# Attention over a few memory slots, then a maxout FFN: four token tiles divided, and a new order of pieces

## The chip, the cores and the metric

The kernel runs on one core of one Trainium2 chip. The metric is the time of one execution on the device in microseconds (us), the median of several runs. Lower is better. A profiled execution gives the trace; its times count from the first instruction (the start of the span).

## The reference, cut to what matters

Eight batches of eight heads, 576 tokens, head size 64, 32 memory slots per head. Keys and values are first gathered into the memory slots, the queries then attend to the slots, and an FFN without biases follows over all 4608 tokens.

```python
a = phi - np.max(phi, axis=2, keepdims=True)
a = np.exp(a)
a = a / (np.sum(a, axis=2, keepdims=True) + 1e-09)
k_m = np.einsum('bhsm,bhsd->bhmd', a, k)
v_m = np.einsum('bhsm,bhsd->bhmd', a, v)
scores = scale * np.matmul(q, k_m.transpose(0, 1, 3, 2))
scores = scores - np.max(scores, axis=-1, keepdims=True)
attn = np.exp(scores)
attn = attn / (np.sum(attn, axis=-1, keepdims=True) + 1e-09)
x = np.matmul(attn, v_m)          # then heads side by side: 4608 x 512
h = np.maximum(np.maximum(x @ w1, x @ w2), x @ w3)
return (h @ w_out).astype(np.float32)
```

## The kernel before

The kernel never forms `x`. The value memory of a batch (32 slots x 64 for each head) is multiplied into the weights, so that attention weights go straight into the FFN. With w1 and w2 the differences to w3 are used: the maximum of three becomes w3's part plus a maximum of two differences and zero, and w3's part reaches the output through w3 @ w_out.

All work is cut into pieces. A piece is a letter, sometimes a number, and a batch: F8@1 is piece F8 of batch 1. A list written out in the code gives the order in which the pieces are issued, and since each engine takes its instructions in program order, the list is the order of every engine's queue. The pieces that matter here:

- L0, L1, L2, L3: the loads of phi, k, v and q of a batch. They are issued by POOL (GpSimd). Loads take eight semaphores in turn, so a load waits until the eighth one before it has landed; it also waits until the buffer (two of each kind) is free. From batch 2 on, r0 and r1 (POOL, L109) copy k and v into a packed buffer.
- E: exp of phi (ACT, L235). B: memory of keys and values on PE (L255, 72 small matmuls); in batches 0 and 1 in two parts, B0 for keys, B1 for values. N: its normalization (DVE, L273 to L287). K: its transposition (PE, L302) and the copy of the result (kvt).
- Q0, Q1: transpositions of q (DVE, L317). S: scores (PE, L337, 32 matmuls) and their exp into e2, in two halves (ACT, L346).
- a, s, c, m, X: for each half of e2, transposition, sum, reciprocal (DVE, L391, L399, L408), multiplication (POOL, L413) and transposition back into `attn` (DVE, L421).
- D0 to D3 (PE, L444): the value memory times the weights ("fold"), copied into `wp` and `wp3` by ACT or DVE, with a star by both. V: the difference of w2 or w1 to w3 (DVE, L219).
- F0 to F11 (PE, L473, four matmuls each): the FFN's first layer for 128 features of one of the two differences. An even F is copied with Relu into `h1` (mostly ACT, L176), the odd F after it is combined with it into `hT` (DVE, L486).
- T0 to T4 (PE, L504 and L513): the second layer for 128 tokens: six matmuls on `hT` and two on `attn`, then a copy into `ot` (ACT or DVE) and an output transfer of 256 KB issued by SP (L534). T4 joins the halves of two batches; T3 of the last batch is done in two parts.

A mark "!" behind a piece gives its copy to the other of ACT and DVE.

PSUM has eight banks. A string of digits in the code names the bank for each piece in turn: one bank for a T or a K, two for a B, D or F, two times two for an S. A piece can start when the last reader of its bank is done.

The first part of the list, up to F4@0, does the start: warming matmuls, the memory of batch 0, the products of the weights. Behind it the tiles of batch 0 stand among the pieces of batch 1, those of batch 1 among the pieces of batch 2, and so on. Before the change a T is one piece, and the order in which its matmuls go through `hT` is that in which the odd F of the batch were issued (`fts`).

Of the kernel before, what the change touches and what calls it, by code (L numbers as in the profile page):

```python
# [15 lines left out]
def kernel(  # L16
# [24 lines left out]
    FT = DF // P  # L41
# [97 lines left out]
    for i in range(P // M):  # L139
# [4 lines left out]
    banks = iter(  # L144
        "".join(
            """
            02010240624567676476420642064204624062453605040462041642062402640150646025126026
            40246024076024764206560260426406246023062414216420640240624042612640234024620460
            24620462352604620520640260240640264204024601460424323232
            """.split()  # L150
        )
    )
# [1 line left out]
    def one_bank():  # L154
        return psum[:, int(next(banks))]
# [166 lines left out]
    attns = {}  # L322
# [137 lines left out]
    hts = {}  # L460
    fts = {}
# [28 lines left out]
                op=ALU.max,  # L490
            )

    osts = {}

    def ffn2(b, t, swap):


        hT, attn = hts[b // 2], attns[b // 2]
        c0 = S - HP if t == 4 else (b % 2) * (S + HP) + t * P
        if b == B - 1 and t == 3:  # L500
            return ffn2_last(b, c0)
        po = one_bank()
        for n, fc in enumerate(fts[b]):
            nc.tensor.matmul(  # L504
                po,
                lhsT=hT[:, fc, c0 : c0 + P],
                rhs=wo_sb[:, fc, :],
                start=(n == 0),
                stop=False,
            )  # L510
# [19 lines left out]
        ot = opool.tile([P, DM], FP32, name="ot")  # L530
        r0 = (b // 2) * 2 * S + c0
        rows = out[r0 : r0 + P, :]
        evacuate("T", t, swap, ot, po)
        nc.sync.dma_start(out=rows, in_=ot)  # L534

    def ffn2_last(b, c0):

        hT, attn = hts[b // 2], attns[b // 2]
        ot = opool.tile([P, DM], FP32, name="ot")
        r0 = (b // 2) * 2 * S + c0  # L540
        for i in range(2):
            c = (slice(0, DM - P), slice(DM - P, DM))[i]
            po = one_bank()[:, 0 : c.stop - c.start]
            for n, fc in enumerate(fts[b]):
                nc.tensor.matmul(  # L545
                    po,
                    lhsT=hT[:, fc, c0 : c0 + P],
                    rhs=wo_sb[:, fc, c],
                    start=(n == 0),
                    stop=False,  # L550
                )
            for g in range(NG):
                nc.tensor.matmul(
                    po,
                    lhsT=attn[:, g, c0 : c0 + P],
                    rhs=wp3s[b][:, g, c],
                    start=False,
                    stop=(g == NG - 1),
                )
            rows = out[r0 : r0 + P, c]  # L560
            if i == 0:
                nc.vector.tensor_copy(out=ot[:, c], in_=po)
                nc.sync.dma_start(out=rows, in_=ot[:, c])
            else:
                nc.scalar.copy(out=ot[:, c], in_=po)
                nc.scalar.dma_start(out=rows, in_=ot[:, c])

    def issue(b, n, swap):

        i = int(n[1:]) if len(n) > 1 else None  # L570
        {
            "I": lambda: [make_identity(nc, ident)]
            + [nc.gpsimd.memset(x[:, :, :, 2 * D : 2 * D + 1], 1.0) for x in kvrs],
            "Y": lambda: load_w(i) if i < 3 else load_wo(),
            "L": lambda: load_ph(b) if i == 0 else load_q(b) if i == 3 else load_kv(b, i - 1),
            "H": lambda: load_kv(b, i % 2, halves[i // 2]),
            "r": lambda: pack(b, i),
            "E": lambda: [att_exp(b, h) for h in (halves if b == 0 else [slice(0, NP)])],
            "B": lambda: att_kv(b, i),
            "N": lambda: att_kv_norm(b, i),  # L580
            "K": lambda: att_kv_t(b, swap, i),
            "Q": lambda: att_q(b, i),
            "S": lambda: att_score(b),
            "a": lambda: att_t(b, i),
            "s": lambda: att_sum(b, i),
            "c": lambda: att_rec(b, i),
            "m": lambda: att_mul(b, i, swap == "!"),
            "X": lambda: (ones_mul if (b, i) in ONES else att_back)(b, i),
            "M": lambda: ones_sum(b, i),
            "R": lambda: ones_rec(b, i),  # L590
            "D": lambda: fold(b, i, swap),
            "F": lambda: ffn1(b, i, swap),
            "T": lambda: ffn2(b, i, swap),
            "W": lambda: w3_t(i, swap),
            "O": lambda: w3_o(i, swap),
            "V": lambda: w_diff(i),
            "Z": lambda: warm_up(i),
        }[n[0]]()


    for w in """
        E@0 H2@0 H0@0 L3@0 Z25@0 B0@0 I@0 N0@0 Z2@0 K0@0! Q0@0 Q1@0 Z9@0 S@0 Z2@0 M0@0 M1@0 R0@0
        Y2@0 R1@0 W0@0 Y3@0 W1@0 W2@0 Z6@0 O1@0 H3@0 O3@0 O2@0 H1@0 X1@0 B1@0 X0@0 N1@0 K1@0
        O0@0 Y0@0 D1@0! D0@0! D3@0 F8@0 F10@0 F2@0 V0@0 F6@0 F0@0! Y1@0 D2@0 D4@0 L0@1 V1@0 F4@0
        F3@0 E@1 L1@1 F5@0 F11@0 F1@0 F7@0 F9@0 L3@1 B0@1 N0@1 L2@1 L1@2 Q0@1 Q1@1 T0@0 V2@0
        K0@1! T3@0 S@1 a0@1 T1@0 a1@1 L2@2 s0@1 L0@2 B1@1 N1@1 L3@2 c0@1 K1@1 m0@1 s1@1 c1@1
        D1@1* D0@1 m1@1 X0@1 X1@1 D2@1! L2@3 D3@1* T2@0 F8@1 L0@3 F10@1 L1@3 F6@1 r0@2 r1@2
        F4@1! F2@1 F9@1 F5@1 F0@1 E@2 F3@1 F11@1 F7@1 F1@1 L3@3 B@2 L2@4 T2@1! L1@4 N@2 K@2!
        T1@1 Q0@2 Q1@2 S@2 L0@4 T4@1! L3@4 a0@2 s0@2 c0@2 r1@3 a1@2 D1@2! E@3 m0@2 s1@2 c1@2
        D0@2* m1@2 D2@2 X0@2 X1@2 T0@1 T3@1 F10@2 F2@2 F6@2 F3@2 F7@2 F0@2 F11@2 r0@3 L1@5 F1@2  # L610
        Q0@3 D3@2 B@3 F8@2 N@3 F9@2 r1@4 F4@2 F5@2 L2@5 K@3! Q1@3 T2@2! S@3 D0@3 a0@3 r0@4 s0@3
        a1@3 E@4 T3@2 c0@3 s1@3 c1@3 T0@2! m0@3 D2@3* D1@3* m1@3 X1@3 L0@5 B@4 D3@3 T1@2 X0@3
        N@4 F6@3 F4@3 Q0@4 L0@6 F8@3 Q1@4 F5@3 F9@3 F0@3 F7@3 F2@3 F1@3 L3@5 F3@3 K@4! F10@3
        L3@6 F11@3 S@4 E@5 T3@3 a0@4 T0@3! L2@6 r0@5 a1@4 s1@4 s0@4 c0@4 r1@5 c1@4 m0@4 D2@4*
        B@5 D1@4! X0@4 D0@4* m1@4 L1@6 X1@4 L1@7 T1@3 F6@4 F4@4 N@5 K@5! F2@4 F8@4! F5@4 L2@7
        F10@4 L0@7 Q0@5 F7@4 Q1@5 F0@4 F1@4 F11@4 T2@3 S@5 F3@4 r1@6 F9@4 a1@5 s1@5 L3@7 T4@3
        E@6 c1@5 Q1@6 m1@5 a0@5 X1@5 D3@4 r0@6 D3@5* D1@5! s0@5 c0@5 T2@4! T3@4 Q0@6 D2@5* D0@5
        m0@5 B@6 T0@4! r0@7 N@6 X0@5 K@6 F10@5 F4@5! F2@5 F11@5 r1@7 F3@5 F6@5! F8@5 F5@5 F7@5
        F9@5 Q0@7 E@7 F0@5 F1@5 T1@4! S@6 B@7 D1@6! a0@6 N@7 s0@6 T3@5 K@7 Q1@7 T0@5 S@7 a1@6
        c0@6 s1@6 D3@7 c1@6 a1@7 m0@6 T1@5 s1@7 D2@6* m1@6 D0@6* D2@7 a0@7 X0@6 s0@7 T4@5! D1@7!  # L620
        c0@7 D0@7! X1@6 c1@7 m1@7 D3@6* T2@5! m0@7 F6@6 F10@6 X1@7 F7@6 F4@6 F0@6! X0@7 F8@6
        F2@6 F11@6 F5@6 F9@6 F4@7 F1@6 F8@7 F3@6 F6@7! T1@6! F5@7 F0@7! F1@7 F2@7 T0@6! T3@6
        F10@7 F7@7 F11@7 F3@7 T2@6 F9@7 T0@7! T1@7! T2@7 T4@7! T3@7
    """.split():
        n, b = w.rstrip("!*").split("@")
        issue(int(b), n, w[-1])
# [30 lines left out]
```

## Time and profile before

| | |
|---|---|
| median of 3 runs | 165.16 us (164.99 to 165.55) |
| the profiled execution | 165.26 us |
| its span, first to last instruction | 163.5 us |
| PE busy | 154.2 us (94%) |
| DVE, ACT, POOL busy | 108.7, 87.0, 69.5 us |
| granted TensorE clock | 1.0 |
| HBM read, written | 39.32, 9.44 MB |

PE is TensorE's matmuls, DVE VectorE, ACT ScalarE, POOL GpSimd, SP SyncE, which issues the outputs. Ends of matmuls are modelled, so PE's pace is read from the starts. In a row of the list in order of time stand the start and the length in us, the engine, the line, what is written and read, and how many instructions are merged; in brackets the idle time of the engine before it and what ended it.

### The profile page before, as it was taken

The numbers are of one execution on the slowest core, as the hardware profiler recorded it, in microseconds if no ns is written. First come the engines' busy times: TensorE is split into PE (matmuls) and PEld (weight loads), VectorE is DVE, ScalarE is ACT, GpSimd is POOL, SyncE is SP. The second block draws the span as 40 slices with busy tenths as digits, with TensorE's granted clock in tenths as the row PEclk, the third lists the DMA queues.
The fourth block names the chain that finished last, engine by engine and source line by source line (L and its number), as shares of the span: only waits on it lengthen the run. The fifth ranks groups of instructions, "written<-read, shape, count | busy, mean of one in ns | idle before, by whom it ended". The sixth has DMA issues, their size and how long they took to land.

```text
span 163.5 us, 4854 instructions
## 1 busy us (share of the span) xinstructions
PE 154.2 (94%) x2080; PEld 85.7 (52%) x2080; DVE 108.7 (66%) x208; ACT 87.0 (53%) x136; POOL 69.5 (42%) x71
## 2 busy tenths in 40 slices
PE   7997698999899999999999999999999999999990
PEld 2342444664467435754674585357653377655440
DVE  2032702899889764876978859996988978727211
ACT  4205325943475288659868683774565975041110
POOL 7931133100399688087685844597002250000000
PEclk9999999999999999999999999999999999999999
DMA  5999999999999999999999999999113130031333
GB/s 152 151 201 209 206 210 214 276 207 210 235 333 227 291 235 262 248 297 219 250 348 268 219 252 233 236 302 271 34 66 130 68 130 0 22 108 66 128 131 127
DMA packets 21974, 31.77 MB, mean 194 GB/s; under 512 B 1216, under 2 KB 16576, under 8 KB 21952
## 3 DMA queue, kind: packets, MB, share of 16 engines
q0 software_dynamic: 16080, 21.43, 68.3%
q1 hardware_dynamic: 5728, 9.96, 17.4%
q8 instruction: 16, 0.26, 0.6%
q10 hardware_dynamic: 144, 0.07, 0.1%
q14 instruction: 6, 0.05, 0.1%
HBM read 39.32 MB, written 9.44 MB: 298 GB/s over the span
## 4 chain that ended last, share of the span: by engine, by line
PE 82%; DMA 7%; ACT 3%; DVE 2%; POOL 2%; issue 1%; POOLq 0%; ACTq 0%; DVEq 0%
PE psum L504 29%; PE psum L473 27%; PE psum L513 8%; DMA w_sb<-in_moe_w_dram 7%; PE psum L444 5%; PE psum L255 4%; PE psum L198 3%; PE psum L337 2%; ACT wp L178 1%; PE psum L522 1%; ACT h L176 1%; PE psum L302 1%; POOL kvo L103 1%; DVE w3T L182 1%; PE psum L545 1%
## 5 line engine op out<-in xcount | busy, mean ns | idle before, releaser
L504 PE MATMUL psum<-wo_sb,hT 128*128 128x512 bf16 x210 | 51.3, 380 | 0.1
L473 PE MATMUL psum<-attn,wp 128*128 128x288 bf16 x384 | 49.9, 286 | 0.2
L473 PEld LDWEIGHTS <-wp 128*128 128x128 bf16 x384 | 36.9, 98 | 12.4 <-ACT wp L178 0.8
L486 DVE TENSOR_TENSOR hT<-psum,h 128x576 bf16<-128x576 f32 x48 | 34.2, 748 | 8.5 <-PE psum L473 7.7
L176 ACT ACTIVATE h<-psum 128x576 bf16<-128x576 f32 x40 | 24.8, 655 | 13.4 <-PE psum L473 13.3
L504 PEld LDWEIGHTS <-hT 128*128 128x128 bf16 x210 | 19.1, 97 | 23.7 <-issue 4.1
L413 POOL TENSOR_TENSOR t<-t,sm 128x576 bf16<-128x576 bf16 x14 | 16.0, 1153 | 33.4 <-DVE sm L408 33.3
L109 POOL COPY kvr<-kvo 128x2304 bf16<-128x2304 bf16 x12 | 25.2, 2113 | 9.7 <-DMA kvo<-in_v_dram 5.4
L178 ACT COPY ot<-psum 128x512 f32<-128x512 f32 x24 | 14.1, 588 | 25.7 <-PE psum L513 15.2
L178 ACT CAST wp<-psum 128x1024 bf16<-128x1024 f32 (+1 forms) x18 | 17.5, 979 | 1.9 <-PE psum L444 1.9
L513 PE MATMUL psum<-wp,attn 128*128 128x512 bf16 x62 | 18.4, 379 | 0.0
L165 PE MATMUL psum<-warm 128*128 128x512 bf16 x44 | 13.1, 455 | 1.2 <-DVE warm L134 1.2
L346 ACT ACTIVATE e<-psum 128x576 bf16<-128x576 f32 x16 | 9.6, 651 | 8.7 <-PE psum L337 8.7
L317 DVE STREAM_TRANSPOSE qT<-qq 128x576 f32<-128x576 f32 x16 | 11.8, 754 | 0.7 <-DMA qq<-in_q_dram 0.7
L182 DVE COPY ot<-psum 128x512 f32<-128x512 f32 x11 | 7.5, 680 | 5.7 <-PE psum L513 4.9
L235 ACT ACTIVATE e<-ph 128x1152 bf16<-128x1152 f32 (+1 forms) x9 | 9.6, 1065 | 1.8 <-DMA ph<-in_phi_dram 1.6
L399 DVE TENSOR_REDUCE sm<-t 128x18 f32<-128x576 bf16 x14 | 10.3, 738 | 0.2
L116 POOL DMA_DIRECT2D qq<-in_q_dram x8 | 6.0, 751 | 10.0 <-DMA w_sb<-in_moe_w_dram 6.9
L513 PEld LDWEIGHTS <-attn 128*128 128x128 bf16 x62 | 6.1, 98 | 7.0
L391 DVE STREAM_TRANSPOSE t<-e 128x288 f32<-128x288 f32 x14 | 6.5, 463 | 4.4 <-ACT e L346 4.3
L103 POOL DMA_DIRECT2D kvo<-in_v_dram x9 | 6.7, 751 | 5.6 <-DMA wo_sb<-in_moe_w_out_dram 3.1
L103 POOL DMA_DIRECT2D kvo<-in_k_dram x9 | 7.0, 775 | 4.3 <-DMA qq<-in_q_dram 2.3
(60 smaller groups left out, 136.6 us busy)
## 6 DMA issues: line engine op xcount, KB each, us to landing
out_dram<-ot SPq DMA_DIRECT2D x35, 256.0 KB, 5.6
qq<-in_q_dram POOLq DMA_DIRECT2D x8, 576.0 KB, 14.2
ph<-in_phi_dram POOLq DMA_DIRECT2D x7, 576.0 KB, 17.2
kvo<-in_k_dram POOLq DMA_DIRECT2D x7, 576.0 KB, 15.7
kvo<-in_v_dram POOLq DMA_DIRECT2D x7, 576.0 KB, 16.3
w_sb<-in_moe_w_dram POOLq DMA_DIRECT2D x3, 768.0 KB, 19.6
wo_sb<-in_moe_w_out_dram POOLq DMA_DIRECT2D x1, 768.0 KB, 15.2
ph<-in_phi_dram SPq DMA_DIRECT2D x2, 288.0 KB, 3.0
```

What stands on the lines that cost most here:

```text
L103: nc.gpsimd.dma_start(out=kv_of(b, i)[:, h].rearrange("p j c d -> p j (c d)"), in_=by_pair((k, v)[i], b)[:, h],)
L109: nc.gpsimd.tensor_copy(out=kvrs[b % 2][:, :, :, D * i : D * (i + 1)], in_=kv_of(b, i))
L165: nc.tensor.matmul(po[:, 0:BANK], lhsT=warm[:, 0:P], rhs=warm, start=True, stop=True)
L176: nc.scalar.activation(out=out_, in_=in_, func=AF.Relu)
L178: nc.scalar.copy(out=out_, in_=in_)
L317: nc.vector.transpose(out=s["qT"][:, j].rearrange("p j c r e -> p (j c r e)").bitcast(FP32), in_=loaded[b]["q"][:, j].rearrange("p j c d - ...
L399: nc.vector.tensor_reduce(out=sm, in_=s["t", g].rearrange("p n r e -> p n e r"), op=ALU.add, axis=mybir.AxisListType.X,)
L413: (nc.vector if swap else nc.gpsimd).tensor_tensor(out=t, in0=t, in1=s["sm", g].unsqueeze(2).to_broadcast([P, S // HP, R, 2]), op=ALU.mult,)
L473: nc.tensor.matmul(acc[:, h, 0:SH], lhsT=wps[b][:, g, w * DF + ft * P : w * DF + (ft + 1) * P], rhs=attn[:, g, c0 : c0 + SH], start=(g == ...
L486: nc.vector.tensor_tensor(out=hT[:, ft, (b % 2) * S : (b % 2 + 1) * S].rearrange("p (h n) -> p h n", h=2), in0=a, in1=s["h1", ft], op=ALU.max,
L504: nc.tensor.matmul(po, lhsT=hT[:, fc, c0 : c0 + P], rhs=wo_sb[:, fc, :], start=(n == 0), stop=False,)
L513: nc.tensor.matmul(po, lhsT=attn[:, g, c0 : c0 + P], rhs=wp3s[b][:, g, :], start=False, stop=(g == NG - 1),)
```

## The change

A new piece p does two of the six matmuls on `hT` of a tile; its PSUM bank stays open until T does what is left. It is used for T0 to T3 of batch 0, whose six matmuls on `hT` are all done in p pieces; their T does the two on `attn`, the copy and the output. Behind F4@0 the list is written anew for all batches, loads and marks included, and with it the banks.

```diff
@@ banks
-            02010240624567676476420642064204624062453605040462041642062402640150646025126026
+            02010240624567676276240624062402640267404502507062062402604620462372467420724062
...
-    osts = {}
-
-    def ffn2(b, t, swap):
+    begun = {}
+
+    def ffn2_part(b, t, count):
 
-
-        hT, attn = hts[b // 2], attns[b // 2]
+        hT = hts[b // 2]
         c0 = S - HP if t == 4 else (b % 2) * (S + HP) + t * P
-        if b == B - 1 and t == 3:
-            return ffn2_last(b, c0)
-        po = one_bank()
-        for n, fc in enumerate(fts[b]):
+        if (b, t) not in begun:
+            begun[b, t] = (one_bank(), 0)
+        po, done = begun[b, t]
+        assert len(fts[b]) >= done + count
+        for n in range(done, done + count):
+            fc = fts[b][n]
             nc.tensor.matmul(
                 po,
                 lhsT=hT[:, fc, c0 : c0 + P],
...
                 start=(n == 0),
                 stop=False,
             )
+        begun[b, t] = (po, done + count)
+        return po
+
+    def ffn2(b, t, swap):
+
+
+        attn = attns[b // 2]
+        c0 = S - HP if t == 4 else (b % 2) * (S + HP) + t * P
+        if b == B - 1 and t == 3:
+            return ffn2_last(b, c0)
+        po = ffn2_part(b, t, FT - begun.get((b, t), (None, 0))[1])
...
+            "p": lambda: ffn2_part(b, i, 2),
...
-        F3@0 E@1 L1@1 F5@0 F11@0 F1@0 F7@0 F9@0 L3@1 B0@1 N0@1 L2@1 L1@2 Q0@1 Q1@1 T0@0 V2@0
-        K0@1! T3@0 S@1 a0@1 T1@0 a1@1 L2@2 s0@1 L0@2 B1@1 N1@1 L3@2 c0@1 K1@1 m0@1 s1@1 c1@1
-        D1@1* D0@1 m1@1 X0@1 X1@1 D2@1! L2@3 D3@1* T2@0 F8@1 L0@3 F10@1 L1@3 F6@1 r0@2 r1@2
-        F4@1! F2@1 F9@1 F5@1 F0@1 E@2 F3@1 F11@1 F7@1 F1@1 L3@3 B@2 L2@4 T2@1! L1@4 N@2 K@2!
-        T1@1 Q0@2 Q1@2 S@2 L0@4 T4@1! L3@4 a0@2 s0@2 c0@2 r1@3 a1@2 D1@2! E@3 m0@2 s1@2 c1@2
-        D0@2* m1@2 D2@2 X0@2 X1@2 T0@1 T3@1 F10@2 F2@2 F6@2 F3@2 F7@2 F0@2 F11@2 r0@3 L1@5 F1@2
-        Q0@3 D3@2 B@3 F8@2 N@3 F9@2 r1@4 F4@2 F5@2 L2@5 K@3! Q1@3 T2@2! S@3 D0@3 a0@3 r0@4 s0@3
...
+        F3@0 F1@0 F11@0 L1@1 F7@0 F9@0 p2@0 p3@0 F5@0 E@1 B0@1 N0@1 L3@1 Q1@1 Q0@1 p3@0 p1@0
+        V2@0 L2@1 p3@0 K0@1! L2@2 p2@0 L1@2 p1@0 p2@0 S@1 a0@1 L0@2 L3@2 s0@1 p0@0 T3@0 a1@1
+        B1@1 p0@0 T2@0! p1@0 c0@1 N1@1 K1@1! L3@3 s1@1 p0@0 L1@3 D1@1! c1@1 m0@1 X0@1 m1@1 D0@1*
+        X1@1 r1@2 D2@1* r0@2 T0@0! T1@0! F8@1 F0@1! F4@1 F5@1 F2@1 F9@1 F6@1 F1@1 F3@1 E@2 F10@1
+        F7@1 F11@1 D3@1 B@2 N@2 Q1@2 T2@1! L2@3 K@2 T4@1! Q0@2 S@2 L0@3 Q1@3 a0@2 L1@4 s0@2 L2@4
+        a1@2 c0@2 L0@4 m0@2 s1@2 c1@2 X0@2 T1@1! T3@1 D0@2* m1@2 D1@2! D2@2 X1@2 L3@4 T0@1! F8@2
+        F4@2 F2@2! r0@3 Q0@3 r1@3 L1@5 F10@2 F11@2 E@3 F3@2 r0@4 F6@2 F5@2 F7@2 D3@2 B@3 N@3
+        F0@2 F9@2 F1@2 K@3! T2@2 D0@3* L2@5 S@3 a0@3 T1@2 E@4 s0@3 L0@5 a1@3 s1@3 r1@4 c0@3 T3@2
...
-        F2@6 F11@6 F5@6 F9@6 F4@7 F1@6 F8@7 F3@6 F6@7! T1@6! F5@7 F0@7! F1@7 F2@7 T0@6! T3@6
-        F10@7 F7@7 F11@7 F3@7 T2@6 F9@7 T0@7! T1@7! T2@7 T4@7! T3@7
+        F10@7 F4@6 F5@7 F3@7 F0@7 F5@6 T1@6 F8@7 F9@7 T3@6 F6@7! F11@7 F1@7 F7@7 T2@6 T4@7 T0@7!
+        T2@7! T1@7 T0@6! T3@7!
```

In the part that is left out, T1@4 stands between D1@5 and F2@5 in the new order, and the copies of F2@5, F6@5, F8@5 are on DVE.

More of the change, by code (lines that the diff above doesn't have):

```diff
@@ L146 @@
             """
-            02010240624567676476420642064204624062453605040462041642062402640150646025126026
-            40246024076024764206560260426406246023062414216420640240624042612640234024620460
-            24620462352604620520640260240640264204024601460424323232
+            02010240624567676276240624062402640267404502507062062402604620462372467420724062
+            46024602401426016240602460246204260423406240140264026420426420642026402462042642
+            06462054062426052604506420640642062462046406042601010101
             """.split()
@@ L610 @@
-        D0@2* m1@2 D2@2 X0@2 X1@2 T0@1 T3@1 F10@2 F2@2 F6@2 F3@2 F7@2 F0@2 F11@2 r0@3 L1@5 F1@2
-        Q0@3 D3@2 B@3 F8@2 N@3 F9@2 r1@4 F4@2 F5@2 L2@5 K@3! Q1@3 T2@2! S@3 D0@3 a0@3 r0@4 s0@3
[L612 to L621, printed above, removed]
@@ new lines @@
+        F7@1 F11@1 D3@1 B@2 N@2 Q1@2 T2@1! L2@3 K@2 T4@1! Q0@2 S@2 L0@3 Q1@3 a0@2 L1@4 s0@2 L2@4
+        a1@2 c0@2 L0@4 m0@2 s1@2 c1@2 X0@2 T1@1! T3@1 D0@2* m1@2 D1@2! D2@2 X1@2 L3@4 T0@1! F8@2
+        F4@2 F2@2! r0@3 Q0@3 r1@3 L1@5 F10@2 F11@2 E@3 F3@2 r0@4 F6@2 F5@2 F7@2 D3@2 B@3 N@3
+        F0@2 F9@2 F1@2 K@3! T2@2 D0@3* L2@5 S@3 a0@3 T1@2 E@4 s0@3 L0@5 a1@3 s1@3 r1@4 c0@3 T3@2
+        m0@3 D1@3* c1@3 X0@3 m1@3 D3@3* B@4 D2@3 T0@2! X1@3 N@4 L3@5 F4@3! F10@3 Q0@4 F6@3 Q1@4
+        K@4! F11@3 L1@6 L0@6 F8@3 L2@6 F9@3 F5@3 F0@3 F7@3 F2@3 F1@3 S@4 F3@3 a0@4 r0@5 a1@4
@@ new lines @@
+        s0@4 r1@5 c0@4 E@5 s1@4 T1@3! c1@4 m1@4 T0@3! D0@4* D2@4* B@5 L3@6 N@5 m0@4 Q0@5 Q1@5
+        D1@4! X0@4 D3@4 T2@3! K@5! T4@3! S@5 L1@7 X1@4 L2@7 F0@4! F6@4 F7@4 F4@4 r0@6 a1@5 F1@4
+        F8@4 s1@5 F2@4 F9@4 c1@5 F10@4 L0@7 a0@5 F5@4 s0@5 E@6 F11@4 T3@3 c0@5 F3@4 D0@5* D2@5
+        r1@6 m0@5 B@6 D1@5* X0@5 T1@4 m1@5 X1@5 N@6 F2@5! F8@5! F10@5 F6@5! F4@5 L3@7 F11@5 F7@5
+        r0@7 K@6! Q1@6 r1@7 F3@5 F5@5 F0@5 T3@4! E@7 Q0@6 D0@6* D3@5 B@7 D3@6* T2@4! N@7 Q1@7
+        F9@5 S@6 K@7! Q0@7 a1@6 T0@4! S@7 a0@6 F1@5 a0@7 T4@5! s1@6 c1@6 a1@7 D0@7 s1@7 D2@6!
@@ L624 @@
+        s0@6 D3@7 s0@7 c0@6 c1@7 T0@5! D1@6! D2@7 m1@6 D1@7 m0@6 T3@5 c0@7 m0@7 X0@6 X1@6 T1@5
+        F10@6! F11@6 F6@6! F2@6 m1@7 X0@7 F7@6 X1@7 F8@6 T2@5 F0@6! F9@6 F1@6 F2@7 F3@6 F4@7
+        F10@7 F4@6 F5@7 F3@7 F0@7 F5@6 T1@6 F8@7 F9@7 T3@6 F6@7! F11@7 F1@7 F7@7 T2@6 T4@7 T0@7!
+        T2@7! T1@7 T0@6! T3@7!
     """.split():
```

## The prediction

> **What bounds the kernel now.** I read the page first, then who waited for whom on PE, then the start in order of time.
>
> ```profile
> span 163.5 us, 4854 instructions
> ...
> PE 154.2 (94%) x2080; PEld 85.7 (52%) x2080; DVE 108.7 (66%) x208; ACT 87.0 (53%) x136; POOL 69.5 (42%) x71
> ...
> DMA  5999999999999999999999999999113130031333
> ...
> PE 82%; DMA 7%; ACT 3%; DVE 2%; POOL 2%; issue 1%; POOLq 0%; ACTq 0%; DVEq 0%
> ```
>
> PE is busy for 94% of the span and carries 82% of the chain that ended last; the transfers (DMA, in 40 slices of 4.1 us) are full until about 114 us. The change touches nothing before F3@0, so what it can win is PE time lost after 32 us. The list of waits from 28 us to the end has two rows on PE:
>
> ```profile
> PE psum L302 <- DVE kvn L277: 0.4, 1, 0.4
> PE psum L444 <- DVE kvt L182: 0.3, 1, 0.3
> ```
>
> Both belong to batch 1's value part (B1@1, N1@1, K1@1, D1@1). In order of time (start, length, engine, line, out<-in, count; in brackets the idle time before), the stretch in which the tiles of batch 0 run:
>
> ```profile
> 31.56 3.92 PE L473 MATMUL psum<-attn,wp 128*128 128x288 bf16 x28
> ...
> 32.84 4.21 DVE L486 TENSOR_TENSOR hT<-psum,h 128x576 bf16<-128x576 f32 x6
> ...
> 35.41 0.80 PE L255 MATMUL psum<-kvo,e 64*32 64x128 bf16 x72
> ...
> 36.15 1.47 PE L504 MATMUL psum<-wo_sb,hT 128*128 128x512 bf16 x6
> ...
> 37.69 1.43 DVE L317 STREAM_TRANSPOSE qT<-qq 128x576 f32<-128x576 f32 x2
> ...
> 39.61 1.20 DVE L219 TENSOR_TENSOR w_sb<-w_sb 128x2048 bf16<-128x2048 bf16 x1
> ...
> 40.41 1.20 ACT L346 ACTIVATE e<-psum 128x576 bf16<-128x576 f32 x2
> ...
> 42.06 0.75 PE L255 MATMUL psum<-kvo,e 64*32 64x64 bf16 x72
> ...
> 42.89 0.29 DVE L277 TENSOR_TENSOR kvn<-psum,rden 128x128 bf16<-128x128 f32 x1
> ...
> 43.24 0.23 PE L302 MATMUL psum<-ident,kvn 128*128 128x128 bf16 x1 [0.43 <-DVE kvn L277]
> ...
> 43.79 0.84 PE L444 MATMUL psum<-w_sb,kvt 64*32 64x512 bf16 x24 [0.32 <-DVE kvt L182]
> ...
> 44.45 0.40 PE L444 MATMUL psum<-w3o,kvt 64*32 64x512 bf16 x8
> ...
> 44.78 1.15 POOL L413 TENSOR_TENSOR t<-t,sm 128x576 bf16<-128x576 bf16 x1 [0.18 <-DVE sm L408]
> ...
> 45.97 0.48 DVE L421 STREAM_TRANSPOSE attn<-t 128x288 f32<-128x288 f32 x1 [0.35 <-POOL t L413]
> ...
> 46.62 1.63 PE L473 MATMUL psum<-attn,wp 128*128 128x288 bf16 x12
> ```
>
> Here PE loses time three times. The seven F pieces from 31.56 to 35.41 take 3.85 us; eight such pieces take 4.05 later (row at 63.70, below), so about 0.3 us went in waiting for the last fold's copy. B1@1 starts at 42.06, and K1@1, the next thing on PE, at 43.24: a B piece takes 0.74 (35.41 to 36.15), so 0.44 is lost. K1@1, one small transposition, holds PE from 43.24 to 43.79; of these 0.55 us the row shows 0.32 as waiting, and since a matmul's end is modelled and the next may start before it, I count 0.5. Together 1.25 us (1.05 with the 0.32). Why it stands there: V2@0 is queued on DVE (39.61) and q's transpositions before it, so batch 1's normalization comes late, and no matmul is left to put in between. After 46 us the list of PE's waits is empty. So 1.25 us is all that a new order can take out of waits.
>
> **The change, part by part.**
>
> *The divided tiles.* Four tiles of batch 0 have six matmuls on hT each; 24 matmuls become 12 p pieces, in the same order and each bank started and finished as before. No matmul is added. A T piece is 1.7 us (36.15 row and its two matmuls more), of which a p is 0.43. Two p stand behind F9@0 and need only the first two hT results: DVE makes the six in 4.21 us from 32.84, 0.70 each, so the second is there at 34.3, and PE, without its 0.3 us hole, comes to p2@0 at 34.5. F1@0 and F11@0 are in front of F5@0 now, so the copy it waits for is done. B0@1 then comes at 35.9, K0@1 at 37.9 as before: DVE sets it (six hT results until 37.05, then the normalization). S@1 comes at 39.35, as q's transpositions end at 39.12; it was 39.8. Between S@1 and D1@1 now lie four p, T3@0's and T2@0's ends and B1@1. N1@1 is done at about 42.7 and K1@1 is reached at 42.6; a p behind it (0.43) covers the copy of kvt. Both holes go. Cost of the division: nothing on PE, since a p's neighbours are full-array matmuls or the same changes of kind that a T had (19 entries into B, S or D pieces after F3@0, in both orders). The other end of the price, that each resumed group loses 0.1 us, would be 1.2 for twelve resumptions; I take zero, as 512-column matmuls of different lines follow each other in the row at 36.15 without a break. Gain here: 1.25.
>
> *The next chain, earlier.* e2 of batch 1 can start at 39.9 rather than 40.41, since no tile copy stands ahead of it on ACT. But V2@0 (1.20) stands ahead of the first a@1 on DVE, until 40.3. The first a@1 had its half of e2 at 41.0 and has it at 40.5 now. From there to the end of X1@1 (45.97 + 0.48 = 46.45) it was 5.45 us, with a wait for B1@1's result and K1@1's copy on DVE in between; now there is half a fold's copy instead of these. I take 4.95 (bounds 4.5 and 5.45, as before): X1@1 ends at 45.45. F8@1 needs it; PE reaches the matmul that does at 46.62 - 1.25 - 0.45 (D3@1, 44.45 to T2@0 at 44.90, is moved behind F11@1) + 0.24 (two matmuls) = 45.15. So 0.3 of the gain goes again (bounds 0 and 0.8; nothing covers it). B@2 has the same work ahead of it as before and comes 0.95 earlier than the 52.63 below: 51.7.
>
> *The loads.* POOL's order of loads changes, and POOL issues them in order. L3@3 and L1@3 move ahead of m0@1; what they wait for (the readers of qq and kvo of batch 1) is done by 40, and m0@1 needs POOL only at 42.5: free. But r1@2 and r0@2 now stand before L2@3 and L0@3, so those are issued at about 50, not 46, and stand in the transfer queue behind q and k of batch 3. It is not starved: q of batch 2 and those two are 9 us of transfers. Issues, each with the answer that has its us to landing:
>
> ```profile
> 20.54 0.74 POOL L103 DMA_DIRECT2D kvo<-in_v_dram  x1 [3.12 <-DMA wo_sb<-in_moe_w_out_dram]
> kvo<-in_v_dram POOLq DMA_DIRECT2D x1, 576.0 KB, 20.0
> 22.20 0.74 POOL L103 DMA_DIRECT2D kvo<-in_k_dram  x1 [0.93 <-PE psum L198]
> kvo<-in_k_dram POOLq DMA_DIRECT2D x1, 576.0 KB, 21.2
> 25.45 0.74 POOL L103 DMA_DIRECT2D kvo<-in_v_dram  x1 [2.51 <-PE psum L255]
> kvo<-in_v_dram POOLq DMA_DIRECT2D x1, 576.0 KB, 23.2
> 27.37 0.75 POOL L100 DMA_DIRECT2D ph<-in_phi_dram  x1 [1.17 <-DMA w_sb<-in_moe_w_dram]
> ph<-in_phi_dram POOLq DMA_DIRECT2D x1, 576.0 KB, 22.6
> 39.72 3.40 SPq L534 DMA_DIRECT2D out_dram<-ot  x3
> 46.67 0.76 POOL L100 DMA_DIRECT2D ph<-in_phi_dram  x1
> ph<-in_phi_dram POOLq DMA_DIRECT2D x1, 576.0 KB, 11.3
> ```
>
> Issue plus time to landing: 40.5, 43.4, 48.7 and 50.0, and phi of batch 3 at 58.0. A load of k, q or v takes 2.9, phi 1.3, and the three output tiles from 39.72 on pushed the one at 48.7 back by 2.3, 0.8 each. In the new order only two output tiles go out before 46, so phi of batch 2 lands at about 49.3; then come q2, q3, k3, v3, phi 3: 4 x 2.9 + 1.3 = 12.9, and four to six output tiles, 3.2 to 4.8. Phi 3 lands between 65.4 and 67.0; I take five tiles, 66.2. That is 8 us later than before. Who waits for it:
>
> ```profile
> 52.63 0.80 PE L255 MATMUL psum<-kvr,e 64*32 64x129 bf16 x72
> ...
> 60.96 1.18 ACT L235 ACTIVATE e<-ph 128x1152 bf16<-128x1152 f32 x1
> ...
> 63.70 4.11 PE L473 MATMUL psum<-attn,wp 128*128 128x288 bf16 x32
> ...
> 64.45 1.74 ACT L176 ACTIVATE h<-psum 128x576 bf16<-128x576 f32 x3
> ...
> 67.75 0.41 PE L444 MATMUL psum<-w3o,kvt 64*32 64x512 bf16 x8
> ...
> 67.97 0.83 PE L255 MATMUL psum<-kvr,e 64*32 64x129 bf16 x72
> ```
>
> E@3 (60.96 here, 1.18 long) stands on ACT before F6@2's copy now, and that copy frees the bank of B@3. PE would come to B@3 at 67.97 - 0.95 + 0.49 (nine F pieces of batch 2 ahead of it, not eight) = 67.5. E@3 from 66.2 to 67.4 and the copy (1.74 / 3 = 0.58) give 67.95: 0.45 is lost (with L the landing, L - 65.75: bounds 0 and 1.25).
>
> The Trainium skill (DMA: Bandwidth & Descriptors, Queues, rings and completion order) says that each engine takes turns between the queues that have work, a packet at a time, so an output tile would take its share as soon as it is issued. The rows differ in part: the load at 43.4 came 2.9 behind the last although two output tiles had been issued at 39.7 to 40.6. By the page alone the sixth tile would count too, phi 3 would land at 67.0, and the sum would end 0.8 higher.
>
> *All later pieces.* The work is the same, in another order. DVE is the tightest:
>
> ```profile
> 100.87:111.24 10.37, 10.37 (x173) 5.05 (x158) 9.31 (x20) 7.14 (x10) 8.56 (x6) 1.00 1.16 262
> ```
>
> It is busy for 9.31 of 10.37 us with no PE time lost. In the new order batch 5's chain lies among all twelve F pieces of batch 4: from F0@4 to the copy of D0@5, on which T1@4's bank hangs, DVE has about 9.5 us of work and PE 9.2. That may cost 0 to 0.4; different neighbours of B and D pieces may give as much back (PE's pieces add up to 0 to 0.4 less). I let them cancel. The end is the same kind of tile after tile with a two-part T3@7: no change.
>
> **Sum.** The profiled execution took 165.26, its span is 163.5; the median of the runs is 165.16. -1.25 + 0.3 + 0.45 = -0.5: 164.8 for such an execution, 164.7 for the median. A measurement of this kernel tells about 0.3%, 0.5 us, from no change.
>
> **Rivals.**
> *Nothing is given back* (0.22): phi 3 lands by 65.4 and X1@1 is in time; -1.25, and up to -0.4 from the neighbours: 163.8. For it: before, PE waited for no load after 46. Against it: E@3 would be in time by nothing.
> *All is given back* (0.15): phi 3 lands at 66.7, five and a half tiles behind; 0.3 + 0.95 = 1.25, and the time is 165.2. For it: the transfers are the one resource besides PE that is full there.
> *Slower through the load of phi 3* (0.18): its place behind v of batch 3, and POOL's copies ahead of its issue, put it at 67.0 (six tiles) to 67.8 (seven): +0.3 to +1.1, 165.8 in the middle. It decides from a landing at 67.2. Against it: seven tiles are all that batch 0 and batch 1 have sent by 61.
> *Banks* (within the last two): up to four of eight banks are held open from 34.5 to 45, so S@1 takes all the others and B1@1 must wait for e2's first half. The Trainium skill (Perfetto Trace Analysis, Optimization Strategy) says that repeating gaps on the saturated engine can mean too little PSUM for the next tile. Here e2's first half ends at 40.5 and B1@1 comes at 40.55; ACT late by one tile copy would cost 0.6 there.
>
> **Numbers.** My forecast has 0.45: 164.7, its own range 164.2 to 165.2; half of it, 0.23, lies lower by over 0.3%. Faster by over 0.3%: 0.23 + 0.22 = 0.45. Slower: 0.15 of the third case and 0.03 of the second = 0.18, and 0.02 for what stands in none of them: 0.2. Within: 0.35. The range 163.7 to 165.8 leaves out half of the third rival and what stands in none.
>
> **What would show it.** Right: K1@1 and D1@1 without a wait, F8@1 at about 45, B@2 near 51.7; ACT idle before E@3 with the phi load named; PE waiting before B@3. Wrong: waits on PE at the p pieces or on a bank at S@1 and B1@1; B@3 at 67.5 or earlier (then nearer 164.0), or after 69 (then slower); a wait of PE at T1@4 or F2@5 of over 0.5.

## The result

The changed kernel takes 164.58 us (median of 21 runs, 164.10 to 165.51) against 165.16 of the kernel before on the same chip; the ratio is 0.9956 (95% interval 0.9941 to 0.9971), so it is faster by 0.44%, 0.73 us by the ratio. All ratios here are of undisturbed runs and the medians of all runs, so the two can differ; most in the row of phi 3 one load later, whose ratio rests on two of six executions (168.12 and 169.59 us) and whose profile is of a longer one (170.85 us). The profiled execution took 164.31 us.

Two lines of the changed kernel's page:

```profile
span 162.5 us, 4830 instructions
...
PE 152.3 (94%) x2058; PEld 86.0 (53%) x2080; DVE 108.6 (67%) x207; ACT 87.2 (54%) x137; POOL 69.6 (43%) x71
```

PE is busy for the same share of the span. Its count is 2058 matmuls of the 2080 whose weight loads are there: 22 records are missing, and its busy time is short by them. So the only waits that the list shows on PE from 28 us to the end are gaps where a record is missing (groups of six with five recorded), and nothing waited there:

```profile
PE psum L505 <- issue: 0.6, 4, 0.2
```

Both waits of before, K1@1's and D1@1's, are gone. The start in order of time:

```profile
31.31 3.11 PE L473 MATMUL psum<-attn,wp 128*128 128x288 bf16 x24
...
39.24 0.49 PE L337 MATMUL psum<-qT,kvt 32*32 32x288 bf16 x32
...
40.63 0.75 PE L255 MATMUL psum<-kvo,e 64*32 64x64 bf16 x72
...
42.62 0.22 PE L302 MATMUL psum<-ident,kvn 128*128 128x128 bf16 x1
...
43.20 0.84 PE L444 MATMUL psum<-w_sb,kvt 64*32 64x512 bf16 x24
...
44.70 0.48 DVE L421 STREAM_TRANSPOSE attn<-t 128x288 f32<-128x288 f32 x1
44.84 6.18 PE L473 MATMUL psum<-attn,wp 128*128 128x288 bf16 x48
...
51.18 0.83 PE L255 MATMUL psum<-kvr,e 64*32 64x129 bf16 x72
```

Here are F4@0, S@1, B1@1, K1@1 with a p behind it, D1@1, X1@1, the twelve F of batch 1 and B@2. F4@0 starts at 31.31, in the profile of before at 31.56; the pieces ahead of it are the same in both kernels, so this 0.25 is not the change's (in the ten other profiles of the same start it comes between 31.08 and 32.50). Two executions are therefore compared from F4@0 on.

Each B of a later batch is a mark on PE, and what work stands ahead of it in each list can be counted; by the starts, a T is 1.73, an F 0.49, an S 0.41, a D 0.22. The marks B@4 to B@7 and the two-part last tile, before and then after:

```profile
77.47 0.85 PE L255 MATMUL psum<-kvr,e 64*32 64x129 bf16 x72
90.61 0.85 PE L255 MATMUL psum<-kvr,e 64*32 64x129 bf16 x72
108.58 0.83 PE L255 MATMUL psum<-kvr,e 64*32 64x129 bf16 x72
119.36 0.80 PE L255 MATMUL psum<-kvr,e 64*32 64x129 bf16 x72
157.77 1.15 PE L545 MATMUL psum<-wo_sb,hT 128*128 128x384 bf16 x6
```

```profile
67.02 0.84 PE L255 MATMUL psum<-kvr,e 64*32 64x129 bf16 x72
76.01 0.85 PE L255 MATMUL psum<-kvr,e 64*32 64x129 bf16 x72
89.38 0.85 PE L255 MATMUL psum<-kvr,e 64*32 64x129 bf16 x72
103.06 0.83 PE L255 MATMUL psum<-kvr,e 64*32 64x129 bf16 x72
113.42 0.83 PE L255 MATMUL psum<-kvr,e 64*32 64x129 bf16 x72
156.75 1.14 PE L557 MATMUL psum<-wo_sb,hT 128*128 128x384 bf16 x6
```

| mark | earlier, as read | work that stands on the other side of it in the new list | gain, less 0.25 |
|---|---|---|---|
| B@2 | 1.45 | none | 1.20 |
| B@3 | 0.95 | one F more ahead (0.49) | 1.19 |
| B@4 | 1.46 | none | 1.21 |
| B@5 | 1.23 | one D more ahead (0.22) | 1.20 |
| B@6 | 5.52 | two T and two D fewer (3.90) | 1.37 |
| B@7 | 5.94 | two T, two F, one S fewer, one D more (4.63) | 1.06 |
| last tile | 1.02 | none | 0.77 |

The gain is made ahead of B@2 and kept through B@5. Up to B@6 some 0.2 is added, and behind B@6 0.6 is lost: 0.4 in all. A piece's price depends on its neighbours (D3@1 took 0.45 ahead of a T before, 44.45 to 44.90, and takes 0.23 ahead of B@2 now, 50.95 to 51.18), so the rows with much moved work are good to 0.1 or 0.2.

### The profile page after: what moved, and what is told of

Read it like the earlier page. It is cut to its first block, busy times and chain, and to the rows that moved or that the text cites. A ratio compares the mean times of both kernels' runs of the same rounds, so it can differ in the third digit from the quotient of the medians.

```text
span 162.5 us, 4830 instructions
## 1 busy us (share of the span) xinstructions
PE 152.3 (94%) x2058; PEld 86.0 (53%) x2080; DVE 108.6 (67%) x207; ACT 87.2 (54%) x137; POOL 69.6 (43%) x71
## 4 chain that ended last, share of the span: by engine, by line
PE 82%; DMA 7%; DVE 2%; issue 2%; POOL 2%; ACT 2%; POOLq 0%; DVEq 0%; ACTq 0%
PE psum L473 28%; PE psum L505 28%; PE psum L525 8%; DMA w_sb<-in_moe_w_dram 7%; PE psum L444 5%; PE psum L255 4%; PE psum L198 3%; PE psum L337 2%; PE psum L534 1%; POOL kvo L103 1%; DVE w3T L182 1%; DVE attn L381 1%; PE psum L302 1%; ACT h L176 1%; PE psum L557 1%
## 5 line engine op out<-in xcount | busy, mean ns | idle before, releaser
L473 PE MATMUL psum<-attn,wp 128*128 128x288 bf16 x384 | 50.7, 286 | 0.3
L505 PE MATMUL psum<-wo_sb,hT 128*128 128x512 bf16 x191 | 49.6, 379 | 1.4 <-issue 0.6
L178 ACT COPY ot<-psum 128x512 f32<-128x512 f32 x27 | 15.9, 589 | 27.9 <-PE psum L525 20.9
L176 ACT ACTIVATE h<-psum 128x576 bf16<-128x576 f32 x36 | 22.8, 658 | 12.1 <-PE psum L473 11.5
L178 ACT CAST wp<-psum 128x1024 bf16<-128x1024 f32 (+1 forms) x18 | 17.0, 979 | 1.7 <-PE psum L444 1.7
L180 DVE TENSOR_SCALAR h<-psum 128x576 bf16<-128x576 f32 x12 | 9.0, 754 | 7.0 <-PE psum L473 6.3
L165 PE MATMUL psum<-warm 128*128 128x512 bf16 x42 | 12.2, 447 | 1.4 <-DVE warm L134 1.2
L178 ACT COPY kvt<-psum 128x384 bf16<-128x384 bf16 (+2 forms) x8 | 3.4, 427 | 10.9 <-PE psum L302 10.9
L255 PEld LDWEIGHTS <-e 64*32 64x32 bf16 x720 | 7.4, 90 | 2.5 <-issue 1.1
```

Of the source, the lines that this page charges most:

```text
L165: nc.tensor.matmul(po[:, 0:BANK], lhsT=warm[:, 0:P], rhs=warm, start=True, stop=True)
L176: nc.scalar.activation(out=out_, in_=in_, func=AF.Relu)
L178: nc.scalar.copy(out=out_, in_=in_)
L255: nc.tensor.matmul(kvp[M * j : M * (j + 1), a, 0:nd], lhsT=s["e"][r, j, c, :], rhs=plain(r, j, c) if b < FULL else kvr[r, j, c, 0:nd], sta ...
L473: nc.tensor.matmul(acc[:, h, 0:SH], lhsT=wps[b][:, g, w * DF + ft * P : w * DF + (ft + 1) * P], rhs=attn[:, g, c0 : c0 + SH], start=(g == ...
L505: nc.tensor.matmul(po, lhsT=hT[:, fc, c0 : c0 + P], rhs=wo_sb[:, fc, :], start=(n == 0), stop=False,)
```

## The experiments

The forecast's theory had three parts: the three holes of PE at the start are worth 1.25; the chain to X1@1 and the later load of phi 3 give some of it back; all later pieces cost nothing. The rivals: more goes at the loads; or the division is not needed, or is all that is needed. All kernels run beside the kernel before.

| run | median us | ratio to before | 95% interval |
|---|---|---|---|
| tiles undivided | 168.10 | 1.0173 | 1.0135 to 1.0211 |
| old order, two pairs | 166.31 | 1.0075 | 1.0052 to 1.0098 |
| the same, other banks | 165.61 | 1.0041 | 1.0022 to 1.0060 |
| new to B@2, then old | 172.48 | 1.0433 | 1.0390 to 1.0477 |
| the same, r1@3 later | 165.85 | 1.0043 | 1.0023 to 1.0062 |
| old to B@2, then new | 174.05 | 1.0555 | 1.0509 to 1.0602 |
| new to B@5, then old | 164.89 | 0.9988 | 0.9970 to 1.0006 |
| old to B@5, then new | 171.33 | 1.0344 | 1.0297 to 1.0390 |
| phi 3 one load later | 171.01 | 1.0230 | 1.0177 to 1.0283 |
| two swaps | 164.39 | 0.9958 | 0.9937 to 0.9978 |

**Is the division needed?** The new order with each tile of batch 0 in one piece, at the place of its last p:

```diff
-  F7@0 F9@0 p2@0 p3@0 F5@0 ... Q0@1 p3@0 p1@0 V2@0 L2@1 p3@0 K0@1! L2@2 p2@0 L1@2 p1@0 p2@0 S@1
+  F7@0 F9@0 F5@0 ... Q0@1 V2@0 L2@1 T3@0 K0@1! L2@2 L1@2 T2@0! S@1
```

> The changed kernel without division: each of the four tiles of batch 0 is one piece, at the place of its last pair (T3@0 before K0@1, T2@0 before S@1, T1@0 before K1@1, T0@0 before D1@1); all else, marks and banks too, as in the changed kernel. Theory 'division': small pieces are what fits into the holes, and it is the ends of T0@0 and T1@0 left for the stretch before F8@1 that cover the chain of batch 1; whole tiles put S@1 0.4 us later, with a tile copy ahead of its exp on ACT, so that F8@1 waits for X1@1 by 0.7 to 1.0 us more: 165.2 to 165.6. Rival 'order': whole tiles at these places cover K1@1's and D1@1's waits as well; 164.6, like the changed kernel, and the division is worth nothing.

It is slower than the kernel before by 1.7%, far more than either theory gave it. From its list of waits on PE, without one ahead of F4@0 and the gaps of missing records:

```profile
PE psum L302 <- DVE kvn L277: 1.1, 1, 1.1
...
PE psum L255 <- ACT e L346: 0.8, 1, 0.8
PE psum L473 <- ACT wp L178: 0.8, 1, 0.8
...
PE psum L473 <- DVE hT L486: 0.3, 1, 0.3
```

Four waits, 3.0 us, all in the stretch that the p pieces fill: F5@0, B1@1, K1@1 and F8@1. From B@2 to B@3 this kernel takes 15.86, the changed one 15.84. From F4@0 to B@2 it takes 23.20, the changed one 19.87. So the whole cost of leaving out the division lies ahead of B@2, and this order of the start works only with it.

**Is the division enough?** The old order, with four matmuls of T2@0 behind B1@1 and K1@1, where PE stood still:

```diff
-  B1@1 N1@1 L3@2 c0@1 K1@1 m0@1 s1@1 c1@1 D1@1*
+  B1@1 p2@0 N1@1 L3@2 c0@1 K1@1 p2@0 m0@1 s1@1 c1@1 D1@1*
```

> The list of before, with one tile divided: two pairs of T2@0 stand behind B1@1 and behind K1@1, where PE waited; the last pair stays at the old place of T2@0. D3@1 is moved behind F10@1 to free a bank, F10@1 takes banks 0 and 1. Theory 'holes are two sided': the waits at K1@1 and D1@1 (0.9 us) go, but X1@1 still ends at about 46.2, so F8@1 waits for it and only 0.2 to 0.5 of them come through: 164.7 to 165.0. Rival 'holes alone': filling the two holes is worth all of 0.9: 164.3.

With 166.31 it is over both forecasts. D3@1 was put behind F10@1 here, and its bank waits 0.8 us for T2@0's copy. That wait comes from D3@1's new place, so a second version has D3@1 behind F1@1 and other banks for it and for F10@1.

> The list of before with two pairs of T2@0 behind B1@1 and K1@1; D3@1 stands behind F1@1 on the banks of F11@1, so that it no longer waits for T2@0's copy (0.8 us in the earlier version). Theory 'holes are two sided': the pairs fill 0.9 us of waits, 0.4 to 0.6 come back before F10@1, since F8@1 and F10@1 wait for batch 1's copies and for X1@1: 164.7 to 164.9. Rival 'bank clash was the whole loss': 164.3. Rival 'division costs': 165.2 or more though no wait for a bank is left.

It is still 0.4% slower than before, and the forecast of a gain fell. Three rows of it:

```profile
43.54 0.84 PE L444 MATMUL psum<-w_sb,kvt 64*32 64x512 bf16 x24
...
45.56 0.40 PE L473 MATMUL psum<-attn,wp 128*128 128x288 bf16 x2 [0.21 <-ACT wp L178]
45.67 0.48 DVE L421 STREAM_TRANSPOSE attn<-t 128x288 f32<-128x288 f32 x1 [0.34 <-POOL t L413]
```

From F4@0 (31.32 in this execution) D1@1 starts 12.22 later, in the kernel before 12.23; X1@1 ends 14.83 later, before 14.89, in the changed kernel 13.87. The p pieces filled the holes, but nothing behind them came earlier: F8@1 now comes too soon and waits for the fold's copy and for X1@1. So the holes were where the lateness of batch 1's chain showed, not its cause. The time is the one that the rival 'division costs' named, but its condition is not met: three waits of 0.2 us each are left on PE, two at F8@1 and one at F6@1. From F4@0 to B@2 it takes 21.38, before 21.07; 0.22 of these 0.31 is D3@1, which before filled time ahead of F8@1 and now stands behind the F pieces. What a resumed group costs is therefore not to be read from this run. In the changed kernel S@1, B1@1 and e2 come sooner, and X1@1 with them by 1.02. That this is what makes its gain fits both runs; no run moves the chain alone.

**Where in the list is the gain made?** Cuts between the two lists. New up to B@2, old behind it, L2@3 and L0@3 behind B@2 as in the new list and E@3 behind F11@2:

> The new list and banks up to B@2 (divided tiles included), then the list and banks of before from B@2 on, with L2@3 and L0@3 right behind B@2 and E@3 moved behind F11@2, since phi of batch 3 now lands at about 64.6. Theory 'start': the change gains about 1.2 us of PE time between F3@0 and B@2 (two holes at K1@1 and D1@1, one at F5@0) and its new order behind B@3 loses 0.4 us again; then this kernel is faster than the changed one: 164.0 us beside 165.16, B@2 at 51.1 and the rest as long as before. Rival 'rest': the divided tiles only move the holes, and the gain is made by the new order of batches 2 to 7; then this one takes 165.2. Rival 'loads': with the new order of loads (q and k of batch 3 ahead of v and phi) the old rest waits for a load in batches 3 to 5, 0.5 to 1.5 us: 164.5 to 165.5, and the trace names a load ahead of PE's or ACT's wait.

The start is as in the changed kernel up to B@2, and then 8 us are lost, far more than any of the three forecasts had. The waits of PE, POOL's queue, and a window behind the wait (its PE busy time, then PEld, DVE, ACT, POOL, the granted clock, DMA's share and GB/s):

```profile
PE psum L473 <- DVE attn L421: 4.0, 2, 3.7
```

```profile
63.71 2.11 POOL L109 COPY kvr<-kvo 128x2304 bf16<-128x2304 bf16 x1 [6.69 <-DMA kvo<-in_v_dram]
65.78 2.27 POOL L413 TENSOR_TENSOR t<-t,sm 128x576 bf16<-128x576 bf16 x2
```

```profile
66.00:70.00 4.00, 2.02 (x8) 1.13 (x9) 1.53 (x3) 0.65 (x1) 4.00 (x3) 0.63 1.20 233
```

The old rest has r1@3, POOL's copy of v of batch 3, ahead of m0@2. With the loads of the new start that v lands near 63.7; m0@2 stands behind the copy in POOL's queue, and all F pieces of batch 2 behind m0@2. And then the granted clock falls, to 0.63 in this window. To show that it is this one piece, it was moved:

```diff
-  a0@2 s0@2 c0@2 r1@3 a1@2 D1@2! m0@2 s1@2 c1@2 D0@2* m1@2 D2@2
+  a0@2 s0@2 c0@2 a1@2 D1@2! m0@2 s1@2 c1@2 D0@2* m1@2 r1@3 D2@2
```

> New list up to B@2 and the old one behind it, as in the first experiment, with one piece moved: r1@3, POOL's copy of v of batch 3, stands behind m1@2 and no longer ahead of m0@2. Theory: the 7.8 us of the first experiment came from POOL's order alone, since m0@2 stood behind a copy that waited for a load; now m0@2 and m1@2 run in time, PE's wait of 4 us before batch 2's F pieces goes, the clock stays at 1.0, and the time is 164 to 165.5. Rival: the load of phi 3 (E@3) or the other loads, late by two places, cost as much by themselves: over 168, with PE waiting at B@3 for ACT's copy behind E@3.

6.6 us come back (165.85, a little over the 165.5 that was expected at most). What is left of the loss has two rows, a bank at the cut (B@2's, which D3@1's copy frees) and v of batch 3:

```profile
52.36 0.81 PE L255 MATMUL psum<-kvr,e 64*32 64x129 bf16 x72 [1.13 <-ACT wp L178]
68.72 0.80 PE L255 MATMUL psum<-kvr,e 64*32 64x129 bf16 x72 [0.84 <-POOL kvr L109]
```

The other way about, old up to B@2 and new behind it:

> The list and banks of before up to B@2, then the new list and banks (nothing is divided). Theory 'start': no gain, and the 0.4 us that the new rest costs: 165.4 to 165.7, with the waits at K1@1 and D1@1 as before. Rival 'rest': 164.5, as the changed kernel.

```profile
65.22 0.78 DVE L317 STREAM_TRANSPOSE qT<-qq 128x576 f32<-128x576 f32 x1 [6.31 <-DMA qq<-in_q_dram]
```

This takes 174.05, far from both forecasts. Here it is DVE's queue: the new rest has Q1@3 ahead of the transposition of e2 of batch 2, and with the old start's loads q of batch 3 lands at 65.2. These cuts say nothing of the parts' worth; they say that the order of loads ahead of B@2 and the order of POOL and DVE behind it belong together.

At B@5 fewer loads are in flight (four in the changed kernel's trace, seven at B@2). New up to B@5, old behind it:

> The new list and banks up to B@5, the list and banks of before from B@5 on; what stood on the other side of the seam is exchanged (T3@3 for T1@3, L3@6 for L1@6, m0@4 for m1@4, D0@4 is done already), so that loads and POOL's copies meet the list that they were ordered for by batch 6. Theory 'start': the gain is made before B@2 and the new list loses about 0.8 us of it behind B@5 (by the starts of weight loads 66.5 us from B@5 to T3@7 against 65.9 in the old one, which does a D piece more): 163.8. Rival 'all one': the lists fit only as wholes and a seam costs 1 us or more wherever it lies, as it did at B@2: 165.5 or more.

```profile
32.35 3.12 PE L473 MATMUL psum<-attn,wp 128*128 128x288 bf16 x24
...
90.44 0.85 PE L255 MATMUL psum<-kvr,e 64*32 64x129 bf16 x72
...
158.09 1.15 PE L557 MATMUL psum<-wo_sb,hT 128*128 128x384 bf16 x6
```

From F4@0 to B@5 it takes 58.09, the changed kernel 58.07. From B@5 to the last tile, with the same work, it takes 67.65, the changed kernel 67.37, and the kernel before 66.94 (67.16 less the D). So the old rest does not bring its own pace to another front; a gain by taking it was expected and not found, and the time lies between the two forecasts. The other cut, old up to B@5:

> Old list up to B@5, new list from B@5 on (the same pieces; the few that lie on different sides of the cut in the two lists are put right behind it). Theory: what the two parts of the list bring adds up. New to B@5 with the old rest came to 0.9988 of before, the whole new list to 0.9956, so the new rest from B@5 on is worth 0.5 us by itself, and this kernel comes to 0.997 of before, 164.6 us, with PE's waits of the start (K1@1, D1@1: 0.4 and 0.3) still there. Rival: the old rest fitted badly only because of the cut (the loads and folds in flight at B@5 differ between the lists), and so does this cut: 165.2 to 165.9, with a new wait on PE within 10 us behind B@5.

```profile
109.32 0.82 PE L255 MATMUL psum<-kvr,e 64*32 64x129 bf16 x72 [3.28 <-POOL kvr L109]
...
110.50 2.74 PE L505 MATMUL psum<-wo_sb,hT 128*128 128x512 bf16 x6
```

L1@6 is issued behind B@5 in this list, so k of batch 6 lands at the end of a full queue; POOL's copies r0@6 and r1@6 follow it, and B@6 waits 3.28 for the second. The time is over both forecasts, and the wait lies further behind the cut than the rival had it. That the two parts' gains add up is neither shown nor refuted by this run.

**How near is the load of phi 3?** The changed kernel with L0@3 moved behind L1@4, by one load of k:

```diff
-  S@2 L0@3 Q1@3 a0@2 L1@4 s0@2
+  S@2 Q1@3 a0@2 L1@4 L0@3 s0@2
```

> The changed kernel with L0@3 issued behind L1@4, one load later. Phi of batch 3 lands at about 69.5 then, not 64.6. Theory of the prediction: E@3 stands on ACT ahead of F6@2's copy, whose bank B@3 needs, so B@3 waits until the landing plus 1.8: PE loses 3.5 to 4 us there, 168.2, and k of batch 4, which lands 1.5 us earlier, gives nothing back. Rival: ACT and PE have other work that can be taken up, or the delay is made good within batch 3 since the later loads are not later: 165 to 166.

```profile
69.80 1.16 ACT L235 ACTIVATE e<-ph 128x1152 bf16<-128x1152 f32 x1 [4.40 <-DMA ph<-in_phi_dram]
...
71.55 1.18 PE L255 MATMUL psum<-kvr,e 64*32 64x129 bf16 x72 [4.06 <-ACT h L176]
```

The mechanism of the third rival stands there: E@3 waits for phi, F6@2's copy stands behind E@3 on ACT, and B@3 waits 4.06 for the bank. By the ratios the time is 2.75% longer than the changed kernel's (1.0230 / 0.9956), 4.5 us, where the theory had 3.5 to 4.

**Can the late loss be taken back?** In the changed kernel F0@5 ahead of F5@5 and F1@5 ahead of S@7, so that F5@5 finds its bank free:

> The changed kernel with two pieces exchanged where PE still loses time behind B@5: F0@5 ahead of F5@5, so that F5@5 does not wait for F11@5's bank (0.3 us), and F1@5 ahead of S@7, so that T4@5 does not wait for F1@5's hT (0.3 us). Theory 'small holes in the rest': 164.0. Rival: the chain from S@7 is 0.5 us later and takes it back further on: 164.6.

The ratio is that of the changed kernel. From B@6 to B@7 it takes 10.30 (10.36 without the swaps), from B@7 to the last tile 43.32 (43.33). It is the best median, and no difference that these runs can tell; the 164.0 of the theory is not reached. F5@5 no longer waits, but F0@5, now in its place, has a bank of K@6, whose copy ends at 109.84; F0@5 starts at 109.89, 0.24 late.

## Why the forecast came out: two misses that cancel

The forecast was -0.5 (-1.25 + 0.3 + 0.45 + 0). The trace shows -0.77, the ratio -0.73.

**The holes, -1.25: right.** K1@1 and D1@1 start without a wait, F5@0 too, and B@2 comes 1.20 earlier, to which F8@1's term has to be added. A resumed group costs nothing that can be seen: twelve resumptions at 0.1 would have left no gain at B@2. With the 0.25 of the start, S@1 came at 39.49 for 39.35 and B1@1 at 40.88 for 40.55; B1@1 did not wait for its bank.

**F8@1's wait, +0.3: too large, it was 0.14.** X1@1 ended at 45.18, with the 0.25 of the start 45.43, and 45.45 was forecast. F8@1's third matmul, which needs it, starts at 45.23; by the pace of the matmuls around it (0.12 each) it would have started 0.14 sooner. PE came to F8@1 0.17 later than thought (44.84 + 0.25 = 45.09 for 44.92): the sum took D3@1 out at 0.45, but some of that goes with the change from a D to a T, whichever D stands there. The four D took 1.11 (43.79 to 44.90), the three that are left take 0.77 (43.20 to 43.97): 0.34 less. So the chain to X1@1 was right, and PE's way to F8@1 was mis-sized.

**The load of phi 3, +0.45: the step that failed; it cost nothing.** Issue and landing of phi of batches 2 and 3, and what stands on ACT and PE:

```profile
27.11 0.75 POOL L100 DMA_DIRECT2D ph<-in_phi_dram  x1 [0.43 <-issue]
ph<-in_phi_dram POOLq DMA_DIRECT2D x1, 576.0 KB, 21.5
49.59 0.76 POOL L100 DMA_DIRECT2D ph<-in_phi_dram  x1
ph<-in_phi_dram POOLq DMA_DIRECT2D x1, 576.0 KB, 15.0
63.15 1.99 ACT L176 ACTIVATE h<-psum 128x576 bf16<-128x576 f32 x3
65.03 1.16 ACT L235 ACTIVATE e<-ph 128x1152 bf16<-128x1152 f32 x1
66.08 0.64 ACT L176 ACTIVATE h<-psum 128x576 bf16<-128x576 f32 x1
```

The order of the queue was right, and so was the place where it would bite. The landing was 64.6, not 66.2; 0.25 of the difference is the earlier start of this execution. Phi 2 came 0.7 sooner (48.6, not 49.3), and between the two lie 16.0, not 16.9: less the 12.9 of the loads, 3.1. Five output tiles land between them (from 49.8 to 62.2), as I took; they cost 0.6 each and not 0.8. ACT goes from the copies of F8@2, F4@2 and F10@2 straight to E@3, and the copy of F6@2, which frees B@3's bank, ends at 66.72, 0.3 ahead of B@3 at 67.02. With the 0.25 B@3 came at 67.27, within the "67.5 or earlier" that the prediction had named as a sign against this step. The rule of the Trainium skill that I weighed there (DMA: Bandwidth & Descriptors, Queues, rings and completion order), by which the engines take turns between queues packet by packet, gave 67.0 with six tiles; the measured landing is 2.4 earlier, and the rows decide. That the engines take turns by packets is not shown by them, nor refuted. The load stands at an edge all the same: one place later in the queue costs 2.75% of the changed kernel's time.

**All later pieces, 0: too small, it was +0.4.** T1@4 and F2@5, where I looked for it, have no wait. Up to B@6 0.17 is won, and 0.6 is lost behind it, in two runs of F pieces. Before, twelve F of batch 5 in a row; after, the ten of batch 5 (with K@6, 0.16, among them), and twelve of batches 6 and 7:

```profile
111.24 6.04 PE L473 MATMUL psum<-attn,wp 128*128 128x288 bf16 x48
117.13 1.46 PE L504 MATMUL psum<-wo_sb,hT 128*128 128x512 bf16 x6
```

```profile
105.79 3.59 PE L473 MATMUL psum<-attn,wp 128*128 128x288 bf16 x28
...
111.15 1.46 PE L505 MATMUL psum<-wo_sb,hT 128*128 128x512 bf16 x5
...
133.60 6.32 PE L473 MATMUL psum<-attn,wp 128*128 128x288 bf16 x48
139.75 1.48 PE L505 MATMUL psum<-wo_sb,hT 128*128 128x512 bf16 x5
```

By the starts an F takes 5.89 / 12 = 0.491 before. The ten would take 5.07 with K@6 and take 5.36; the twelve take 6.15 for 5.89. That is 0.29 and 0.26, and B@7's and the last tile's rows in the table fall by 0.31 and 0.29. Each is one short stop, too short for PE's list of waits; the rows of the weight loads (PEld) show them:

```profile
109.37 1.42 DVE L486 TENSOR_TENSOR hT<-psum,h 128x576 bf16<-128x576 f32 x2 [0.59 <-ACT h L176]
...
110.18 0.83 PEld L473 LDWEIGHTS <-wp 128*128 128x128 bf16 x7 [0.33 <-issue]
...
136.12 2.58 ACT L176 ACTIVATE h<-psum 128x576 bf16<-128x576 f32 x4 [3.50 <-PE psum L473]
136.82 2.79 PEld L473 LDWEIGHTS <-wp 128*128 128x128 bf16 x23 [0.30 <-issue]
```

F5@5 starts at 110.18 and has the banks of F11@5, whose combination on DVE, the first of the two, ends at 110.12. F10@7 starts at 136.82 and has the banks of F2@7, whose copy on ACT, the first of the four, ends at 136.77. The stops are 0.30 and 0.28; the kernel before has none of over 0.04 in its runs of F pieces behind B@2. The first was tried by the swaps, and of its 0.29 only 0.06 came back, since the piece put there met another copy. The kernel with undivided tiles has the same twelve pieces on the same banks and takes 5.88 for them, without the second stop, and from B@7 to the last tile 43.05 for 43.33. So that stop costs what it shows; why F2@7's copy runs late in the changed kernel stays open.

So 0.75 of the gain was forecast to go again, and some 0.5 did, nearly all of it at another place: that the total came out so near is luck. At the loads it went as the first rival had it (nothing is given back, phi 3 in time), and the time is still not the rival's 163.8, because of the late F pieces. The rival through the load of phi 3 did not come about, nor the banks.

## What to carry to other kernels

A hole on the busiest engine is filled for good only if what ends it comes earlier too: pieces put into the same holes of the old order gained nothing, since the next wait was already there. Where a list is rewritten, measure its parts by marks on the busiest engine, corrected for the work that was moved past each mark; this told to 0.1 or 0.2 us where the gain was made and where it went. In an in-order queue a load and all that stands behind its first reader, on POOL and DVE above all, have to be moved together.

## What the runs showed of the hardware

After PE had stood for 3 to 4 us, it was slow for some time. Behind the 3.28 at B@6 above, the six matmuls of a T take 2.74 (1.46 elsewhere), and in the kernel with the cut at B@2 the granted clock of the stretch behind the wait is 0.63. Waits of up to 1.1 us (undivided tiles) left it at 0.9 or more in all slices of the page but the last. The Trainium skill (TensorE: Matmul & The Clock Gate, HAM oscillation — how this bites in real kernels) says that idle gaps of over about 3.4 us bring TensorE back to half its clock. The trace agrees: the 3.28 is counted from a modelled end, and by the starts PE had been free for 3.46 (two D start at 105.42 and take 0.44, B@6 starts at 109.32). It did not come each time: one execution of old to B@5 had a mean clock of 1.0 and took 169.79 us, four others had 0.977 to 0.99 and took 171.0 to 171.8. So a late load can cost more than the wait itself: at the cut at B@2 PE waited 4.0 us for batch 2's F pieces, and moving the one piece brought 6.6 back.
